# Attention and MoE on one core: work units of 256 queries of two heads, MoE by 256 tokens, routing of two heads packed in 32 rows, and a longer normalisation chain on the Pool queue

## The chip, the core and the metric

The kernel runs on one core of a Trainium2 chip. The core has a matrix engine (TensorE, PE in the profile; its weight loads are listed as PEld), a vector engine (VectorE, DVE), a scalar engine (ScalarE, ACT), a general engine (GpSimd, POOL) and a queue engine (SyncE, SP). Each engine takes its instructions strictly in program order and waits on semaphores of the others, so one waiting instruction holds everything behind it on its engine. SP and POOL also issue DMA transfers. The metric is the device time of one execution in microseconds; of several runs the median is given.

## What is computed

Four batches of eight heads, 768 positions, head size 64. Every query and key is assigned to the nearest of 16 centroids of its head; a query sees only the keys of its own cluster. The result goes through one feed-forward block (512 to 2048 to 512, SiLU) over 3072 tokens.

```python
q_assign = np.argmax(np.einsum('bhsd,hcd->bhsc', q_n, c_n), axis=-1)
k_assign = np.argmax(np.einsum('bhsd,hcd->bhsc', k_n, c_n), axis=-1)
mask = q_assign[:, :, :, None] == k_assign[:, :, None, :]
scores = scale * np.matmul(q, k.transpose(0, 1, 3, 2))
scores = np.where(mask, scores, -1000000000.0)
attn = np.exp(scores - np.max(scores, axis=-1, keepdims=True))
attn = attn / (np.sum(attn, axis=-1, keepdims=True) + 1e-09)
x = np.matmul(attn, v).transpose(0, 2, 1, 3).reshape(B * S, H * D)
h = x @ w_in
g = h * (1.0 / (1.0 + np.exp(-h)))
out = g @ w_out
```

## The kernel before

**Pairs.** Work is cut into 16 pairs: pair p holds two neighbouring heads of one batch, four pairs to a batch. For each pair q and k are loaded (`load_qk`, tiles nat0 and nat1, SP queue), split on DVE into two fp16 halves (`split`, tile hl, lines 109 and 110), and turned by a transposing DMA on the SP queue (`turn`, tile abt, line 115), so that positions lie along the free axis and 128 rows (64 high, 64 low) on the partitions.

**Routing.** `logits` (line 127) multiplies with the normalised centroids, 16 small matmuls a pair, whose results lie in PSUM tiles psL in four strips of 32 partitions (head, q or k), of which 16 rows are used. DVE turns them (`route_a`, lines 136 and 137, tile lt), takes the maximum and the one-hot comparison and turns that back (`route_b`, lines 143 to 149), and writes the scaled one-hot rows into partitions 64 to 80 of abt, over the low half (`route_c`, line 156, four DVE operations a pair). A matmul over 80 rows then gives score plus a large bonus where the clusters agree.

**Attention in slots.** The program is written out in slots. In slot s, `qk` makes the scores of one 128-key block of one head against all 768 queries (lines 167 and 168, PSUM tile st, two buffers) and ACT takes the exponential into P (line 170). Six slots later `pv` multiplies P with the values (line 184); the value tile holds 64 columns of ones beside the values, so the sum of the exponentials z comes out in rows of its own. Half of the 768 queries at a time is accumulated in the one PSUM buffer pv and copied by ACT to osb (line 190). 192 slots make up the attention.

**The z chain.** The sums must divide the result: `z_out` spreads one row of osb over 128 partitions (DMA, tile zt), `z_recip` takes the reciprocal on DVE (line 202) and writes it to DRAM (tile rzd), `z_bcast` reads it back to 64 partitions per head (line 210, tile rzb), and `z_mul` multiplies on DVE into xt (line 216). All DMAs of the chain go on the SP queue, the same as all loads, the transposing DMAs and the stores of the output.

**MoE.** When the four pairs of a batch are done, its 768 tokens are two chunks of 384. `unit_a` (line 230, PSUM tile ph; tanh on ACT, line 234; product on DVE, line 235, tile gt) and `unit_b` (line 244, PSUM tile po; scaling on DVE, line 247, tile ot; store) are put into the slots of the next batch's attention, between `qk` and `pv` and behind `pv`. The last batch's MoE stands behind the attention by itself. psL, ph and po share three PSUM buffers.

The order on every engine is the order in which this Python code emits instructions; `events` puts the routing, loads and z chain of each pair at fixed slots.

## Time and profile before

| | |
|---|---|
| three timings | 468.02, 468.89, 471.84 us, median 468.89 us |
| profiled execution | 473.52 us, of which 471.7 us from first to last instruction |
| PE busy | 358.7 us, 76% |
| ACT busy | 259.5 us, 55% |
| DVE busy | 240.3 us, 51% |
| mean granted clock of TensorE | 0.904 |
| largest shares of the chain that ended last | PE 38%, DMA 23% (rzb 16%), DVE 20%, the SP queue 10% |

A row of instructions reads: line, engine, operation, output<-input, count, busy time, mean of one in ns, idle time of the engine ahead of it and what ended that. A row of stages gives, from A to B, the length, then busy us and instruction counts of PE, PEld, DVE, ACT and POOL, the granted clock (1.00 is full speed), the busy share of the DMA engines and GB/s. In a row of the time line the first number is the start, the second the duration. Matmuls overlap in time, so what a stream of them costs is read from the distance of their starts, not from their durations.

### The profile page before, as it was taken

The numbers are of one execution on the slowest core, as the hardware profiler recorded it, in microseconds if no ns is written. First come the engines' busy times: TensorE is split into PE (matmuls) and PEld (weight loads), VectorE is DVE, ScalarE is ACT, GpSimd is POOL, SyncE is SP. The second block draws the span as 40 slices with busy tenths as digits, with TensorE's granted clock in tenths as the row PEclk, the third lists the DMA queues.
The fourth block names the chain that finished last, engine by engine and source line by source line (L and its number), as shares of the span: only waits on it lengthen the run. The fifth ranks groups of instructions, "written<-read, shape, count | busy, mean of one in ns | idle before, by whom it ended". The sixth has DMA issues, their size and how long they took to land.

```text
span 471.7 us, 5345 instructions
## 1 busy us (share of the span) xinstructions
PE 358.7 (76%) x1922; PEld 179.2 (38%) x1922; DVE 240.3 (51%) x432; ACT 259.5 (55%) x387; POOL 23.6 (5%) x52
## 2 busy tenths in 40 slices
PE   0666474745598795959799596949959899979996
PEld 0122231322254352524354252524425455535552
DVE  7735143618284555645376465636159544536451
ACT  2273563927287373926478382835548688506340
POOL 2123000000000000000000000000000000000000
PEclk9997977979699798979979897998989999988999
DMA  6989956282608063442606154260812310120011
GB/s 176 227 168 218 198 143 143 60 201 35 168 0 200 3 143 105 86 138 56 189 24 155 49 107 139 45 182 24 196 50 42 94 58 23 58 79 24 23 46 67
DMA packets 81067, 48.82 MB, mean 103 GB/s; under 512 B 61072, under 2 KB 75408, under 8 KB 81040
## 3 DMA queue, kind: packets, MB, share of 16 engines
q1 hardware_dynamic: 78352, 44.28, 36.8%
q0 software_dynamic: 2688, 4.19, 5.1%
q8 instruction: 15, 0.25, 0.2%
q14 instruction: 12, 0.10, 0.1%
HBM read 33.59 MB, written 6.39 MB: 85 GB/s over the span
## 4 chain that ended last, share of the span: by engine, by line
PE 38%; DMA 23%; DVE 20%; SPq 10%; ACT 4%; issue 4%; DVEq 0%; ACTq 0%
DMA rzb<-rzd 16%; PE ph L230 13%; PE po L244 12%; PE pv L184 6%; SPq L115 4%; DMA abt<-hl 4%; PE st L167 4%; DVE hl L110 3%; DVE gt L235 3%; DMA zt<-osb 3%; SPq L92 2%; SPq L99 2%; DVE abt L156 2%; PE st L168 2%; DVE hl L109 2%
## 5 line engine op out<-in xcount | busy, mean ns | idle before, releaser
L170 ACT ACTIVATE P<-st,bias_74 128x768 f16<-128x768 f32 x192 | 171.5, 903 | 99.6 <-PE st L168 98.7
L234 ACT ACTIVATE tn<-ph,zbias 128x384 f32<-128x384 f32 x128 | 74.4, 582 | 81.4 <-PE ph L230 80.1
L235 DVE SCALAR_TENSOR_TENSOR gt<-tn,ph 128x384 f16<-128x384 f32 x128 | 69.8, 552 | 75.4 <-ACT tn L234 72.9
L244 PE MATMUL po<-wout_s,gt 128*128 128x512 f16 x384 | 100.4, 393 | 0.0
L230 PEld LDWEIGHTS <-win_s 128*128 128x128 f16 x512 | 52.8, 103 | 90.1 <-issue 59.7
L167 PE MATMUL st<-abt 80*128 80x512 f16 x192 | 80.9, 422 | 1.3 <-ACT P L170 0.5
L230 PE MATMUL ph<-xt_70,win_s 128*128 128x384 f16 x128 | 45.2, 353 | 41.4 <-DVE lt L136 19.5
L168 PE MATMUL st<-abt 80*128 80x256 f16 x192 | 56.4, 294 | 0.0
L127 PE MATMUL psL<-abt,wh 128*32 128x512 f16 (+1 forms) x128 | 21.2, 409 | 45.1 <-DMA abt<-hl 43.6
L244 PEld LDWEIGHTS <-gt 128*128 128x128 f16 x384 | 38.6, 101 | 40.9 <-issue 5.6
L230 PE MATMUL ph<-xt_73,win_s 128*128 128x384 f16 x128 | 45.2, 353 | 6.4 <-DVE xt_73 L216 6.4
L230 PE MATMUL ph<-xt_71,win_s 128*128 128x384 f16 x128 | 45.0, 352 | 0.0
L230 PE MATMUL ph<-xt_72,win_s 128*128 128x384 f16 x128 | 44.9, 350 | 0.0
L190 ACT COPY osb<-pv 128x384 f32<-128x384 f32 x64 | 30.6, 478 | 15.6 <-PE pv L184 15.4
L127 PEld LDWEIGHTS <-wh 128*32 128x32 f16 x128 | 6.2, 105 | 58.8 <-issue 55.4
L167 PEld LDWEIGHTS <-abt 80*128 80x128 f16 x192 | 20.3, 106 | 19.8 <-issue 9.6
L168 PEld LDWEIGHTS <-abt 80*128 80x128 f16 x192 | 20.3, 106 | 17.9 <-issue 9.0
L247 DVE TENSOR_SCALAR ot<-po 128x512 f32<-128x512 f32 x24 | 16.4, 684 | 18.4 <-PE po L244 18.2
L216 DVE TENSOR_TENSOR xt_73<-osb,rzb 64x768 f16<-64x768 f32 x8 | 7.6, 953 | 33.3 <-DMA rzb<-rzd 33.2
L156 DVE TENSOR_SCALAR abt<-oh 16x768 f16<-16x768 f16 x64 | 23.3, 364 | 1.6
L184 PE MATMUL pv<-P,vb_80 128*128 128x384 f16 x72 | 19.7, 359 | 1.6 <-ACT osb L190 1.6
L216 DVE TENSOR_TENSOR xt_72<-osb,rzb 64x768 f16<-64x768 f32 x8 | 7.6, 952 | 24.5 <-DMA rzb<-rzd 24.4
(133 smaller groups left out, 297.0 us busy)
## 6 DMA issues: line engine op xcount, KB each, us to landing
natv<-in_v_dram SPq DMA_DIRECT2D x16, 384.0 KB, 3.9
rzb<-rzd SPq DMA_DIRECT2D x32, 192.0 KB, 5.7
out_dram<-ot SPq DMA_DIRECT2D x24, 256.0 KB, 2.0
win_s<-in_moe_w_in_dram POOLq DMA_DIRECT2D x4, 512.0 KB, 8.6
wout_s<-in_moe_w_out_dram POOLq DMA_DIRECT2D x4, 512.0 KB, 9.1
abt<-hl SPq DMA_TRANSPOSE x32, 3.7
zt<-osb SPq DMA_DIRECT2D x32, 3.0 KB, 2.8
nat_91<-in_q_dram SPq DMA_DIRECT2D x1, 384.0 KB, 2.9
```

Source lines behind the costliest of these rows:

```text
L115: nc.sync.dma_start_transpose(abts[p][:, t], hls[p][:, t].rearrange("p a c d -> p (a c d)"))
L127: nc.tensor.matmul(psL[g : g + 32, 0 : hi - lo], w[:, 2 * r + h], ab[:, h, lo:hi], start=(i == 0), stop=(i == 1),)
L156: nc.vector.tensor_scalar(out=ab[64 : 64 + HC, h, :], in0=ohs[p][g : g + HC, :], scalar1=OHV, scalar2=None, op0=ALU.mult)
L167: nc.tensor.matmul(st[:, 0:512], kt[0:K, ts(j, 128)], qt[0:K, 0:512], start=True, stop=True)
L168: nc.tensor.matmul(st[:, 512:768], kt[0:K, ts(j, 128)], qt[0:K, 512:768], start=True, stop=True)
L170: nc.scalar.activation(out=P, in_=st[:, 0:768], func=AF.Exp, bias=bias32, scale=ESC)
L184: nc.tensor.matmul(po[:, 0:CH], vt[:, j, :], Ps[i, j][:, ts(u, CH)], start=(j == 0), stop=(j == NJ - 1))
L190: nc.scalar.copy(osbs[i][:, ts(u, CH)], po[:, 0:CH])
L230: nc.tensor.matmul(ph[:, 0:CH], win_s[:, r, ts(fb, 128)], xts[r][:, T0 : T0 + CH], start=(r == 0), stop=(r == NR - 1))
L234: nc.scalar.activation(out=tn, in_=ph[:, 0:CH], func=AF.Tanh, bias=zbias, scale=0.5)
L235: nc.vector.scalar_tensor_tensor(out=gts[c][:, fb, :], in0=tn, scalar=1.0, in1=ph[:, 0:CH], op0=ALU.add, op1=ALU.mult)
L244: nc.tensor.matmul(po, gts[c][:, fc, ts(s, 128)], wout_s[:, fc, :], start=(fc == 0), stop=(fc == NFB - 1))
```

## The change

**Units.** One unit is now 256 queries of both heads of a pair: 48 units of three slots, 144 slots. A slot makes two key blocks of two heads against 256 queries: four `qk` matmuls of 256 columns, one exponential over 1024 elements, and two slots later four `pv` matmuls of 256 columns. The copy of the result to osb (512 elements) is on DVE instead of ACT. In batches 1 to 3 the query blocks are the outer loop, so the 256 tokens of a block are complete after four units; batch 0 has an order of its own.

**MoE by 256 tokens.** Twelve chunks of 256 tokens. A `unit_a` covers two blocks of 128 hidden features by 256 tokens (eight matmuls of 256 columns, tanh and product over 512 elements); a `unit_b` is as before, four matmuls of 512 columns. A chunk has eight of each. They are spread over the slots until the next chunk is there; the first is there at slot 36, the last at slot 156.

**Routing.** The two heads' centroids are packed into one strip of 32 columns and accumulated together, so two pairs fill the 128 partitions, and DVE works on two pairs at once over 768 elements instead of 384. Only pairs 0 and 1 are done singly. The scaling by OHV is one DVE operation over the whole tile, and the one-hot rows go into abt by DMAs on the SP queue, four a pair, 64 in all.

**The z chain** runs per unit, 48 times: three DMAs on the POOL queue (144 in place of 80 on SP), the reciprocal three slots behind `z_out`, and `z_mul` nine slots behind it.

Loads and routing are placed earlier (`front`): four pairs of the next batch are made ready during this one, with seven abt buffers for four and six value tiles for three. The weights of the MoE, still on the POOL queue, are issued at slots 8 to 14 and 20 to 26, between the z chain's DMAs.

```diff
-    CH = 384
+    U = 3
+    UQ = S // U
...
-    wh = const.tile([128, H, 32], f16, name="wh")
-    wl = const.tile([128, H, 32], f16, name="wl")
-    NV = 3
...
+    wh = const.tile([128, HB, 2, 32], f16, name="wh")
+    wl = const.tile([128, HB, 2, 32], f16, name="wl")
+    NV = 6
+    vts = [const.tile([128, NJ, 2, 128], f16, name=f"vt{n}") for n in range(NV)]
...
-            abts[p] = mp.tile([128, 2, 2 * NJ, 128], f16, name="abt", bufs=4)
...
+            abts[p] = mp.tile([128, 2, 2 * NJ, 128], f16, name="abt", bufs=7)
...
+            for n, (w, h) in enumerate(((wh, 0), (wh, 1), (wl, 0), (wl, 1))):
+                for a, p in enumerate(pl):
                     for t in range(2):
-                        g = 32 * (2 * h + t)
+                        g = 64 * a + 32 * t
...
-    def route_c(p, h):
-        for t in range(2):
-            g = 32 * (2 * h + t)
-            ab = abts[p][:, t].rearrange("p (h j) c -> p h (j c)", h=2)
-            nc.vector.tensor_scalar(
-                out=ab[64 : 64 + HC, h, :], in0=ohs[p][g : g + HC, :], scalar1=OHV, scalar2=None, op0=ALU.mult
...
+        ohu = mp.tile([128, S], f16, name="ohu", bufs=1)
+        nc.vector.transpose(ohu[0:n], oht[0:n])
         oh = mp.tile([128, S], f16, name="oh", bufs=2)
-        nc.vector.transpose(oh, oht.rearrange("p a c -> p (a c)"))
-        ohs[p] = oh
...
+        nc.vector.tensor_scalar(out=oh[0:n], in0=ohu[0:n], scalar1=OHV, scalar2=None, op0=ALU.mult)
+        ohs[pl[0]] = oh
+
+    def route_c(pl):
+        oh = ohs.pop(pl[0])
+        for a, p in enumerate(pl):
+            for h in range(2):
+                for t in range(2):
+                    g = 64 * a + 32 * t + HC * h
+                    ab = abts[p][:, t].rearrange("p (h j) c -> p h (j c)", h=2)
+                    nc.sync.dma_start(ab[D : D + HC, h, :], oh[g : g + HC, :])
...
-            nc.scalar.copy(osbs[i][:, ts(u, CH)], po[:, 0:CH])
...
-        nc.sync.dma_start(zts[p][:, h, :], osbs[i][row : row + 1, :].rearrange("o (p i) -> o p i", i=NJ))
```

The new functions and the new order of the work:

```python
    def qk(n, s, p, u):
        ab = abts[p].rearrange("p t (h j) c -> p t h (j c)", h=2)
        st = ps.tile([128, 2, 2, UQ], f32, name="st", tag="st", bufs=2)
        for a in range(2):
            for h in range(2):
                nc.tensor.matmul(
                    st[:, a, h, :], ab[0:K, 1, h, ts(2 * s + a, 128)], ab[0:K, 0, h, ts(u, UQ)], start=True, stop=True
                )
        P = mp.tile([128, 2, 2, UQ], f16, name="P", bufs=5)
        nc.scalar.activation(out=P, in_=st, func=AF.Exp, bias=bias32, scale=ESC)
        Ps[n, s] = P
    def pv(n, s, p, u):
        if s == 0:
            pvs[n] = ps.tile([128, 2, UQ], f32, name="pv", tag="pv", bufs=1)
        po = pvs[n]
        P = Ps.pop((n, s))
        for a in range(2):
            for h in range(2):
                nc.tensor.matmul(
                    po[:, h, :], vts[p % NV][:, 2 * s + a, h, :], P[:, a, h, :],
                    start=(s == 0 and a == 0 and h == 0), stop=(s == 2 and a == 1), skip_group_check=True,
                )
        if s == 2:
            osb = mp.tile([128, 2, UQ], f32, name="osb", bufs=6)
            nc.vector.tensor_copy(osb, po)
            osbs[n] = osb
    def z_out(n):
        zt = mp.tile([32, 16], f32, name="zt", bufs=2)
        nc.gpsimd.dma_start(zt, osbs[n][D : D + 1].rearrange("o h x -> o (h x)").rearrange("o (p i) -> o p i", p=32))
        zts[n] = zt
    def z_recip(n):
        rz = mp.tile([32, 16], f32, name="rz", bufs=2)
        nc.vector.reciprocal(rz, zts.pop(n))
        rzd = dr.tile([1, 2 * UQ], f32, name="rzd", bufs=4)
        nc.gpsimd.dma_start(rzd.rearrange("o (p i) -> (o p) i", p=32), rz)
        rzs[n] = rzd
    def z_bcast(n):
        rzb = mp.tile([64, 2, UQ], f32, name="rzb", bufs=2)
        nc.gpsimd.dma_start(rzb.rearrange("p h x -> p (h x)"), rzs.pop(n).to_broadcast([64, 2 * UQ]))
        rzbs[n] = rzb
    def z_mul(n, p, u):
        b, r = divmod(p, HB)
        c = b * U + u
        if c not in xts:
            xts[c] = mp.tile([128, NR, UQ], f16, name="xt", bufs=4)
        osb, rzb = osbs.pop(n), rzbs.pop(n)
        for h in range(2):
            nc.vector.tensor_tensor(
                out=xts[c][D * h : D * h + D, r, :], in0=osb[0:D, h, :], in1=rzb[:, h, :], op=ALU.mult
            )
    def unit_a(c, f):
        if f == 0:
            gts[c] = mp.tile([128, NFB, UQ], f16, name="gt", bufs=2)
        ph = ps.tile([128, 2, UQ], f32, name="ph", tag="moe", bufs=3)
        for e in range(2):
            for r in range(NR):
                nc.tensor.matmul(
                    ph[:, e, :], win_s[:, r, ts(2 * f + e, 128)], xts[c][:, r, :], start=(r == 0), stop=(r == NR - 1)
                )
        tn = mp.tile([128, 2, UQ], f32, name="tn", bufs=3)
        nc.scalar.activation(out=tn, in_=ph, func=AF.Tanh, bias=zbias, scale=0.5)
        nc.vector.scalar_tensor_tensor(
            out=gts[c][:, 2 * f : 2 * f + 2, :], in0=tn, scalar=1.0, in1=ph, op0=ALU.add, op1=ALU.mult
        )
...
    units = []
    for b in range(B):
        if b == 0:
            seq = [(0, 0), (0, 1), (0, 2), (1, 0), (1, 1), (2, 0), (2, 1), (3, 0), (3, 1), (1, 2), (2, 2), (3, 2)]
        else:
            seq = [(r, u) for u in range(U) for r in range(HB)]
        units += [(b * HB + r, u) for r, u in seq]
    LAST = 3 * len(units)
    PVL = 2
...
    def front(pl, R):
        x = R - 26
        for p in pl:
            at(x, lambda p=p: (load(p, 0), load(p, 1)))
            at(x + 3, lambda p=p: load_v(p))
            at(x + 9, lambda p=p: split_turn(p, 0))
            at(x + 11, lambda p=p: split_turn(p, 1))
            at(x + 15, lambda p=p: cast_v(p))
            x += 3
        at(R - 8, lambda: logits(pl))
        at(R - 7, lambda: route_a(pl))
        at(R - 6, lambda: route_b(pl))
        at(R - 5, lambda: route_c(pl))
...
    at(9, lambda: logits([2, 3]))
    at(10, lambda: route_a([2, 3]))
    at(11, lambda: (route_b([2, 3]), route_c([2, 3])))
    for n, fn in enumerate(wl_in):
        at(8 + 2 * n, fn)
    for n, fn in enumerate(wl_out):
        at(20 + 2 * n, fn)
    for b in range(1, B):
        front([b * HB, b * HB + 1], 36 * b - 6)
        front([b * HB + 2, b * HB + 3], 36 * b + 5)
    LAG = 11
    done = {}
    for n, (p, u) in enumerate(units):
        e = 3 * n + 3 + PVL
        at(e, lambda n=n: z_out(n))
        at(e + 3, lambda n=n: z_recip(n))
        at(e + 5, lambda n=n: z_bcast(n))
        at(e + LAG - PVL, lambda n=n, p=p, u=u: z_mul(n, p, u))
        done[p // HB * U + u] = e + LAG - PVL
    avail = {}
    for c in range(NC):
        avail.setdefault(done[c] + 1, []).append(c)
...
    def pop_unit():
        if qa and (not qb or flip[0] % 2 == 0):
            c, f = qa.pop(0)
            unit_a(c, f)
            if f == NFB // 2 - 1:
                qb.extend((c, s, t) for s in range(UQ // 128) for t in range(4))
        elif qb:
            unit_b(*qb.pop(0))
        flip[0] += 1
...
    for s in range(END):
        for fn in events.get(s, ()):
            fn()
        for c in avail.get(s, ()):
            qa.extend((c, f) for f in range(NFB // 2))
        nxt = [x for x in slots if x > s]
        until = (nxt[0] if nxt else END) - s
        acc += left() / (until + 1)
        n = int(acc)
        acc -= n
        if s < LAST:
            m, j = divmod(s, 3)
            qk(m, j, *units[m])
        for _ in range(n - n // 2):
            pop_unit()
        if PVL <= s < LAST + PVL:
            m, j = divmod(s - PVL, 3)
            pv(m, j, *units[m])
        for _ in range(n // 2):
            pop_unit()
    while qa or qb:
        pop_unit()
```

**How instructions move, 1: the queues of the z chain.** On SP before, in the middle of the program (batch 1), the chain's DMAs stand among transposes and loads:

```order
L115 DMA_TRANSPOSE abt<-hl 128x12x128
L204 DMA rzd<-rz 128x2x6
L115 DMA_TRANSPOSE abt<-hl 128x12x128
L99 DMA natv<-in_v_dram 128x2x384
L92 DMA nat_1415<-in_q_dram 128x2x384
L92 DMA nat_1417<-in_k_dram 128x2x384
L210 DMA rzb<-rzd 64x768 x2
L198 DMA zt<-osb 128x1x6
```

On POOL now, about the same place; the numbers are those of the buffers, so that `rzb_1606<-rzd_1535` is seen to wait for the third row:

```order
L185 DMA zt_1459<-osb_1444 32x1x16
L197 DMA rzb_1511<-rzd_1457 64x512
L192 DMA rzd_1535<-rz_1533 32x16
L185 DMA zt_1537<-osb_1528 32x1x16
L197 DMA rzb_1606<-rzd_1535 64x512
```

The chain has left the queue of the loads; on its own queue it takes turns, unit by unit, in the order rzd, zt, rzb.

**2: the start of the POOL queue.** Now, from slot 5 to slot 11 (vt are the value tiles, win_s the first MoE weights):

```order
L185 DMA zt_315<-osb_302 32x1x16
L88 CAST vt2_77<-natv_313 128x6x64 x2
L88 CAST vt3_78<-natv_329 128x6x64 x2
L323 DMA win_s_68<-in_moe_w_in_dram 128x2048
L192 DMA rzd_368<-rz_366 32x16
L185 DMA zt_370<-osb_363 32x1x16
L323 DMA win_s_68<-in_moe_w_in_dram 128x2048
L197 DMA rzb_435<-rzd_368 64x512
L192 DMA rzd_468<-rz_466 32x16
```

Before, POOL held only the value casts and the weights; now the first units' chain stands between them.

**3: DVE in the middle of a batch.** Before, ahead of a routing:

```order
L202 RECIPROCAL rz_1847<-zt_1701 128x12
L109 TENSOR_SCALAR hl_1818<-nat1_1648 128x12x64
L110 SCALAR_TENSOR_TENSOR hl_1818<-nat1_1648,hl_1818 128x12x64
L247 TENSOR_SCALAR ot_1884<-po_1828 128x512
L216 TENSOR_TENSOR xt3_73<-osb_1640,rzb_1890 64x768
L216 TENSOR_TENSOR xt3_73<-osb_1768,rzb_1890 64x768
L136 STREAM_TRANSPOSE lt_1951<-psL_1920 128x512
L137 STREAM_TRANSPOSE lt_1951<-psL_1929 128x256
```

Now, about the same place:

```order
L223 SCALAR_TENSOR_TENSOR gt_1927<-tn_2116,ph_2107 128x512
L179 COPY osb_2141<-pv_2081 128x512
L207 TENSOR_TENSOR xt_1950<-osb_1846,rzb_2023 64x256 x2
L190 RECIPROCAL rz_2145<-zt_2060 32x16
L235 TENSOR_SCALAR ot_2218<-po_2132 128x512
L121 STREAM_TRANSPOSE lt_2225<-psL_2173 128x512
L122 STREAM_TRANSPOSE lt_2225<-psL_2190 128x256
L179 COPY osb_2246<-pv_2162 128x512
L129 TENSOR_REDUCE mx_2248<-lt_2225 128x48
L131 TENSOR_TENSOR oht_2250<-lt_2225,mx_2248 128x768
L136 STREAM_TRANSPOSE ohu_2252<-oht_2250 128x768
L138 TENSOR_SCALAR oh_2254<-ohu_2252 128x768
```

The multiplications of the chain are smaller and stand every third slot, further behind the sums they wait for; the copies osb<-pv, ACT's before, now stand in DVE's row, behind the product gt and between the pieces of the routing.

More of the change, by code (lines that the diff above doesn't have):

```diff
@@ L224, in unit_a @@
-    def unit_a(c, fb):
-        T0 = c * CH
-        if fb == 0:
-            gts[c] = mp.tile([128, NFB, CH], f16, name="gt", bufs=2)
-        ph = ps.tile([128, 512], f32, name="ph", tag="moe", bufs=3)
-        for r in range(NR):
-            nc.tensor.matmul(
-                ph[:, 0:CH], win_s[:, r, ts(fb, 128)], xts[r][:, T0 : T0 + CH], start=(r == 0), stop=(r == NR - 1)
-            )
-        tn = mp.tile([128, CH], f32, name="tn", bufs=3)
-        nc.scalar.activation(out=tn, in_=ph[:, 0:CH], func=AF.Tanh, bias=zbias, scale=0.5)
+        nc.vector.tensor_scalar(out=oh[0:n], in0=ohu[0:n], scalar1=OHV, scalar2=None, op0=ALU.mult)
@@ L371 @@
-    LAST = 12 * NP
-    queue = []
-    NSL = LAST + 14
-    for s in range(NSL):
+    for vt in vts:
+        nc.gpsimd.memset(vt[:, :, :, D:128], 1.0)
+    centroid_math(craw)
+    for p in range(2):
+        for t in range(2):
+            split_turn(p, t)
+        if p == 0:
+            load_v(0)
+            cast_v(0)
+    for t in range(2):
+        load(2, t)
+    logits([0])
+    route_a([0])
+    route_b([0])
+    route_c([0])
+    load_v(1)
+    cast_v(1)
+    wl_in = [lambda r=r: nc.gpsimd.dma_start(win_s[:, r], win_v[:, r]) for r in range(NR)]
```

290 lines of the change are left out of this document (87 added, 203 removed).

## The prediction

> **What bounds the kernel now.** I read the stages first: length, busy us of PE, PEld, DVE, ACT, POOL with instruction counts, granted clock, DMA share, GB/s. The first row lies in the attention of batch 0, the next two are the batches with MoE, routing and loads together, the last is attention with MoE, when nothing is left to load or route.
>
> ```profile
> 20.00:66.00 46.00, 28.66 (x137) 12.51 (x132) 16.29 (x28) 25.70 (x35) 8.25 (x14) 0.85 0.96 204
> ...
> 127.80:233.50 105.70, 86.65 (x477) 43.92 (x477) 57.61 (x102) 64.18 (x96) 3.83 (x8) 0.90 0.41 103
> 233.50:345.40 111.90, 88.94 (x480) 45.00 (x480) 58.31 (x103) 64.33 (x96) 3.85 (x8) 0.89 0.40 100
> ...
> 371.00:407.00 36.00, 34.16 (x197) 18.89 (x196) 17.59 (x32) 29.41 (x45) 0.00 (x0) 1.00 0.14 45
> ```
>
> The reader is to see three things. Until 127.8 us no MoE runs, and neither PE nor ACT is full (28.66 and 25.70 of 46), while DMA is (0.96). In the two middle batches PE is busy 82% and 79%, at a clock of 0.90. Without routing and loads PE is busy 95% at full clock: the engine can do it, the waits keep it from it. The list of waits (who waited for whom, us in total, times, longest) names them:
>
> ```profile
> PE psL L127 <- DMA abt<-hl: 43.6, 19, 6.5
> DVE xt_73 L216 <- DMA rzb<-rzd: 33.2, 4, 10.9
> DVE xt_72 L216 <- DMA rzb<-rzd: 24.4, 4, 10.1
> ```
>
> The time line shows what one wait of DVE does:
>
> ```profile
> 254.30 0.86 SPq L99 DMA_DIRECT2D natv<-in_v_dram  x1
> ...
> 256.30 1.12 SPq L210 DMA_DIRECT2D rzb<-rzd  x2
> 262.37 1.94 DVE L216 TENSOR_TENSOR xt_70<-osb,rzb 64x768 f16<-64x768 f32 x2 [4.47 <-DMA rzb<-rzd]
> 265.11 0.48 PE L230 MATMUL ph<-xt_70,win_s 128*128 128x384 f16 x1 [4.81 <-DVE lt L136]
> 265.39 0.53 PE L230 MATMUL ph<-xt_71,win_s 128*128 128x384 f16 x1
> ...
> 269.59 0.33 PE L230 MATMUL ph<-xt_70,win_s 128*128 128x384 f16 x1
> 269.75 0.32 PE L230 MATMUL ph<-xt_71,win_s 128*128 128x384 f16 x1
> ```
>
> The sums' way back (rzb) is issued behind three loads on SP and lands 6.1 us later. DVE stands, the logits' PSUM buffer isn't emptied, PE stands 4.81 us, and then its matmuls start 0.28 us apart instead of 0.16. So the order of the SP and DVE queues bounds the middle, DMA and SP the start.
>
> **The change, part by part.** The sum has four terms. These rows price them: groups by line (busy us, mean ns of one), then the time line, then the chain that ended last.
>
> ```profile
> L170 ACT ACTIVATE P<-st,bias_74 128x768 f16<-128x768 f32 x192 | 171.5, 903 | 99.6 <-PE st L168 98.7
> ...
> L234 ACT ACTIVATE tn<-ph,zbias 128x384 f32<-128x384 f32 x128 | 74.4, 582 | 81.4 <-PE ph L230 80.1
> L235 DVE SCALAR_TENSOR_TENSOR gt<-tn,ph 128x384 f16<-128x384 f32 x128 | 69.8, 552 | 75.4 <-ACT tn L234 72.9
> L247 DVE TENSOR_SCALAR ot<-po 128x512 f32<-128x512 f32 x24 | 16.4, 684 | 18.4 <-PE po L244 18.2
> L156 DVE TENSOR_SCALAR abt<-oh 16x768 f16<-16x768 f16 x64 | 23.3, 364 | 1.6
> L149 DVE STREAM_TRANSPOSE oh<-oht_86 128x768 f16<-128x768 f16 x8 | 7.8, 978 | 0.3
> L216 DVE TENSOR_TENSOR xt_73<-osb,rzb 64x768 f16<-64x768 f32 x8 | 7.6, 953 | 33.3 <-DMA rzb<-rzd 33.2
> 21.05 6.26 ACT L170 ACTIVATE P<-st,bias_74 128x768 f16<-128x768 f32 x7 [16.43 <-PE st L168]
> 30.83 0.27 PE L168 MATMUL st<-abt 80*128 80x256 f16 x1
> 30.94 0.49 PE L184 MATMUL pv<-P,va_79 128*128 128x384 f16 x2
> ...
> 39.89 1.47 PE psL L127 x12
> ...
> 129.96 1.29 PE ph L230 x4
> ...
> 377.50 0.86 PE po L244 x4
> ```
>
> Scaled by elements, as estimates: DVE has 1.03 ns per element (552 at 384, 684 at 512), so gt and the osb copy of 512 take 0.68 us, an xt of 256 takes 0.42. ACT has 0.84 ns (582 at 384, 903 at 768): an exponential of 1024 takes 1.12 us, a tanh of 512 0.69. Four matmuls of 512 columns take 0.86, so 256 columns cost 0.108 us, and the two rows at 30.8 show one of 256 starting its successor 0.11 us later, with a weight load beside it.
>
> *Term 1, up to slot 36, where MoE begins: 97 us.* The first exponential stood at 21.05. Now a single pair's logits use two strips instead of four (1.47 us cold becomes 2.9), the maximum and comparison grow by 384 elements each (0.8), the scaling shrinks by 1.1, and four DMAs must land (zt below: 2.8): 24.5 us. ACT alone would bring slot 36 at 24.5 + 36 x 1.12 = 65 us. DMA does not:
>
> ```profile
> q1 hardware_dynamic: 78352, 44.28, 36.8%
> q0 software_dynamic: 2688, 4.19, 5.1%
> natv<-in_v_dram SPq DMA_DIRECT2D x16, 384.0 KB, 3.9
> win_s<-in_moe_w_in_dram POOLq DMA_DIRECT2D x4, 512.0 KB, 8.6
> zt<-osb SPq DMA_DIRECT2D x32, 3.0 KB, 2.8
> rzd<-rz SPq DMA_DIRECT2D x16, 6.0 KB, 2.5
> ```
>
> q1 moved 44.28 MB in 36.8% of 471.7 us, 0.255 MB/us. By slot 33 (logits of pairs 6 and 7) eight pairs have been loaded (24 x 0.39 = 9.4 MB) and turned (16 x 0.39 = 6.3 MB): 62 us. The weights took 5.1%, 24 us, and twelve rzb of 131 KB take 6: 92 us at a full share, 95 with three more slots, 97 with gaps. If the second half of the weights (12 us), needed only from slot 38, slips behind, it is 85; the upper end is a rival. Before, the first unit_a stood at 130 (row 129.96).
>
> *Term 2, PE from slot 36 on: 267 us at full clock.* 108 slots x 8 matmuls x 0.108 = 93; 96 unit_a x 8 x 0.108 = 83; 96 unit_b x 0.86 = 83; logits of eight pairs, 16 matmuls each, 1.0 us warm by the half of the row at 39.89 (12 in 1.47, cold): 8. The other two engines have less per batch of 36 slots: PE 74 us; ACT 36 x 1.12 + 24 x 0.69 = 57, against 64.3, since the copies leave it; DVE 58.3 as before + 8.2 for twelve copies + 2.5 for 24 small xt instead of 8 + 2 for reciprocals - 5.8 for line 156 - 4 for two wide routings instead of four - 1 = 60. That the clock is full rests on the row 371 to 407, where no wait is long; at 0.90, as in the middle batches, the term is 296. The row at 265.11 shows what lowers it, a wait of 4.81. The Trainium skill (TensorE: Matmul & The Clock Gate, What's actually happening) puts the limit at about 3.4 us of idleness and the low clock at half; by that rule waits of under 1 us leave the term at 267, and the trace agrees with the half (0.28 against 0.16).
>
> *Term 3, waits in that stretch: 22 us.* The z chain leaves the path: nine slots of 2.07 us are 18.6, and POOL's three issues (0.6 each, row below), 2.8, 0.2, 2.5 and at most 6.1 for rzb make 13.6. What is late next is the copy osb<-pv, for there is one pv buffer. If a unit_a stands just before the closing pv, the slot's exponential, tanh, product and copy end 2.4 us after that unit's last matmul (0.3 + 0.7 + 0.7 + 0.7), while PE has 1.7 us of other work (pv 0.43, qk 0.43, one unit 0.86) before it needs the buffer: a wait of 0.7, in about half of 36 units, 14 us. The routing's second part is one piece of 3.3 us on DVE (maximum and comparison over 768 elements 0.95 each by gt's slope, turn 0.98, scaling 0.4), against three shared PSUM buffers: 1 us each, six times. Late zt: 2. Bounds: 5, if the queues run ahead, and the first rival.
>
> *Term 4, the end: 6 us.* The last chunk's 14 us on PE are in term 2. After the last pv nine slots with one unit in each last 9.6 us, the chain of the last unit by the rows of before's end
>
> ```profile
> 413.11 2.03 DMA zt<-osb
> 415.51 2.37 DMA rzd<-rz
> 417.94 3.11 DMA rzb<-rzd
> ...
> 467.64 0.69 DVE ot L247
> ```
>
> and issues and reciprocal of 2 us takes 9.5: 1 to 2 us late. From the start of ot to the span's end it was 4.1.
>
> POOL's chain has also come behind the value casts, which wait for their loads: from batch 1 on those are issued twelve slots earlier, in slots 6 and 7 one slot, which is among the gaps of term 1. SP loses 80 DMAs of the chain and gets 64 of the one-hot rows; what waits behind those are loads and transposes that are needed at least eight slots later: nothing. More buffers: nothing.
>
> Sum: 97 + 267 + 22 + 6 = 392 us of span. The profiled execution lay 1.8 above its span and the median of the timings 1.0% below that: **390 us**.
>
> **The rivals.** *Waits come back on DVE.* It now holds the copies that release pv, the products that release ph, and the routing in longer pieces, at 60 of 74 us. If PE stays at the 80% of the middle batches, term 2 is 334 and the time 434. For it speaks the single pv buffer; against it that those batches' long waits all begin with rzb. 13%.
>
> *The chain behind the weights.* In slots 8 to 14 and 20 to 26 the three legs of the first units queue behind weights on POOL's one queue, at 8.6 us each: 25.8 against the nine slots' 10.1, so some 16 us late, and 9 more in the second burst: 415. The sum holds the weights' DMA time, not this order. 10%; together with the first rival, 459, 4%.
>
> *Slower: the POOL queue sets the pace.* Per unit it issues rzd, zt, rzb, and the next rzd waits for zt and the reciprocal: 0.6 + 0.6 + landing + 0.2.
>
> ```profile
> 23.83 2.38 POOL L340 DMA_DIRECT2D win_s<-in_moe_w_in_dram  x4
> ```
>
> With zt's 2.8 us this is 4.2, under the 6.2 of three slots. POOL's only transfers in this trace, though, land after 8.6: then 10.0 a unit, 47 x 10.0 + 31 for the first + 27 for the last chunk = 528 of span, 525. It decides from a landing of 4.8 us, and is slower than before from 7.4. I take 2.8, since those transfers carry 512 KB and zt 2 KB: 8%. The Trainium skill (DMA: Bandwidth & Descriptors, SWDGE vs HWDGE vs iDMA) says that POOL's descriptors are written to SBUF and are held up while DVE uses both ports; by that rule an issue could take up to a DVE operation more, and the rows show 0.6 with DVE busy, which leaves the chance as it is.
>
> *Weight loads show.* If each of the 1632 matmuls of 256 columns after slot 36 paid its 0.10 load, 163 us more: 551. The rows at 30.8 speak against it, but never with two in a row: 3%.
>
> **How the numbers follow.** Forecast 62%, own range 363 (term 1 85, term 3 5 to 8) to 404 (12 us more). Then 13, 10, 4, 8 and 3%. The range 364 to 436 holds nearly all of the forecast, the second rival and the first: about 81%. 1% is about what a measurement here can tell. Faster 0.87 (62 + 13 + 10 and half of the 4), same 0.02, slower 0.11.
>
> **What would show it.** Right: unit_a's first matmul near 97 us; no wait of xt on rzb over 2 us after that; PE busy over 90% at a clock above 0.97 from there; PE's waits there mostly at pv on osb, under 1 us each. Wrong: waits of rz on zt or xt on rzb in every unit (POOL's pace), ph waiting for gt at 80% PE (DVE), starts of 256-column matmuls 0.2 us apart (weights), or the first unit_a later than 115 us.

## The result, and the profile after

The changed kernel takes 414.38 us (median of four runs, 413.35 to 424.15) beside 470.37 us for the kernel before on the same chip: a ratio of 0.882, with a 95% interval of 0.875 to 0.889. The forecast was 390 us.

The stages of both kernels, cut at the start of the first `unit_a` (columns: from and to in us, length, busy us and count of PE, PEld, DVE, ACT and POOL, granted clock, DMA share, GB/s). First before:

```profile
20.00:130.00 110.00, 65.81 (x331) 29.92 (x326) 47.32 (x80) 60.68 (x83) 11.13 (x20) 0.84 0.67 150
130.00:471.70 341.70, 288.42 (x1564) 147.77 (x1562) 178.10 (x312) 195.92 (x302) 8.64 (x18) 0.92 0.32 83
```

and then the changed kernel:

```profile
24.00:130.30 106.30, 61.98 (x396) 38.57 (x397) 46.59 (x80) 38.45 (x36) 27.34 (x50) 0.68 0.88 164
130.30:422.40 292.10, 274.67 (x2150) 201.32 (x2147) 182.39 (x337) 177.31 (x205) 67.81 (x132) 0.99 0.36 98
```

The reader is to see that the whole gain lies behind the first `unit_a`. That stretch fell from 341.7 to 292.1 us, with PE busy 94% of it at a clock of 0.99. Of the 49.6 us, 35.9 are PE's idle time (53.3 before, 17.4 now) and 13.7 its busy time. The first `unit_a` itself stands at 130.3 us, where it stood before (130.0), although it should have come at 97. The profiled execution is some 10 us above the median of its runs (that of the rerun below some 6); the variants below have 284 to 290 us behind their first `unit_a` where nothing is changed there, so in a run at the median it would start at about 124 us (an estimate: 414.4 - 1.8 around the span - 289).

What PE waited for behind the first `unit_a` before (130 to 471 us; us in total, times, longest):

```profile
PE ph L230 <- DVE lt L136: 19.5, 5, 5.4
...
PE ph L230 <- DVE gt L235: 12.4, 3, 6.1
PE ph L230 <- DVE ot L247: 9.1, 2, 4.8
```

and what waited for what there in the changed kernel:

```profile
PE pv L173 <- DVE osb L179: 7.5, 10, 1.8
PE ph L218 <- DVE xt L207: 2.6, 1, 2.6
...
DVE xt L207 <- DMA rzb<-rzd: 1.0, 2, 0.8
```

The waits of the products for rzb, up to 10.9 us each before, are gone, and with them PE's long waits for DVE at ph. This is read from the traces: no run took back one part of the change alone, so how much of the 49.6 us is due to the chain's own queue, to its longer distance, to the larger units or to the packed routing is not shown. The time line shows PE there as a gapless stream, four matmuls of 256 columns every 0.44 us, eight in 0.87:

```profile
260.11 0.60 PE L173 MATMUL pv<-P,vt_77 128*128 128x256 f16 x4
260.55 0.60 PE L158 MATMUL st<-abt 80*128 80x256 f16 x4
260.99 1.04 PE L218 MATMUL ph<-xt,win_s 128*128 128x256 f16 x8
```

In the first stage (24 to 130.3 us) the same list reads otherwise:

```profile
ACT P L162 <- PE st L158: 87.0, 19, 20.9
...
PE pv L173 <- DVE osb L179: 31.9, 11, 6.6
...
DVE xt L207 <- DMA rzb<-rzd: 16.9, 4, 7.3
DVE lt L121 <- PE psL L111: 16.3, 3, 6.6
...
PE psL L111 <- DMA abt<-hl: 9.9, 6, 4.6
```

ACT waits for PE, PE for DVE's copy of the sums, DVE for rzb and for logits, the logits for transposes. PE stands 44.3 of the 106.3 us and works the other 61.98 at a clock of 0.68, so at full clock the work would be about 42 us (an estimate: 61.98 x 0.68). That makes the stage 42 us of work, 20 us of low clock and 44 us of waits. What holds it was the question of the experiments.

### The profile page after: what moved, and what is told of

It is laid out like the page before. It is cut to its first block, busy times and chain, and to the rows that moved or that the text cites. A ratio compares the mean times of both kernels' runs of the same rounds, so it can differ in the third digit from the quotient of the medians.

```text
span 422.4 us, 6704 instructions
## 1 busy us (share of the span) xinstructions
PE 340.9 (81%) x2562; PEld 241.7 (57%) x2562; DVE 243.2 (58%) x454; ACT 218.6 (52%) x243; POOL 100.9 (24%) x196
## 4 chain that ended last, share of the span: by engine, by line
PE 50%; DMA 17%; DVE 17%; issue 7%; ACT 3%; SPq 2%; POOL 2%; ACTq 0%; DVEq 0%; POOLq 0%
PE po L232 17%; PE ph L218 12%; PE pv L173 9%; PE st L158 8%; DMA rzd<-rz 7%; DMA abt<-hl 5%; PE psL L111 3%; DVE gt L223 3%; DVE osb L179 3%; DVE hl L93 2%; ACT tn L222 2%; DMA abt<-oh 2%; DVE hl L94 2%; SPq L99 2%; DMA zt<-osb 2%
## 5 line engine op out<-in xcount | busy, mean ns | idle before, releaser
L162 ACT ACTIVATE P<-st,bias_70 128x1024 f16<-128x1024 f32 x144 | 158.6, 1112 | 155.1 <-PE st L158 153.8
L158 PE MATMUL st<-abt 80*128 80x256 f16 x576 | 94.3, 289 | 9.1 <-DMA abt<-oh 8.8
L218 PE MATMUL ph<-xt,win_s 128*128 128x256 f16 x768 | 98.5, 275 | 3.7 <-DVE xt L207 2.6
L223 DVE SCALAR_TENSOR_TENSOR gt<-tn,ph 128x512 f16<-128x512 f32 x96 | 63.7, 670 | 41.1 <-ACT tn L222 40.9
L222 ACT ACTIVATE tn<-ph,zbias 128x512 f32<-128x512 f32 x96 | 65.6, 684 | 36.6 <-PE ph L218 36.6
L192 POOL DMA_DIRECT2D rzd<-rz x48 | 25.5, 531 | 150.1 <-DVE rz L190 149.9
L179 DVE COPY osb<-pv 128x512 f32<-128x512 f32 x48 | 32.9, 685 | 31.8 <-PE pv L173 31.8
L197 POOL DMA_DIRECT2D rzb<-rzd x48 | 25.7, 535 | 104.5 <-DMA rzd<-rz 100.4
L207 DVE TENSOR_TENSOR xt<-osb,rzb 64x256 f16<-64x256 f32 x96 | 39.6, 413 | 18.6 <-DMA rzb<-rzd 17.9
L173 PE MATMUL pv<-P,vt_77 128*128 128x256 f16 x108 | 19.1, 307 | 10.3 <-DVE osb L179 10.3
L173 PE MATMUL pv<-P,vt_75 128*128 128x256 f16 x108 | 18.1, 295 | 9.5 <-DVE osb L179 9.5
L173 PE MATMUL pv<-P,vt_78 128*128 128x256 f16 x108 | 17.5, 288 | 9.9 <-DVE osb L179 9.9
L173 PE MATMUL pv<-P,vt_76 128*128 128x256 f16 x108 | 17.5, 288 | 7.1 <-DVE osb L179 7.1
```

Source lines behind the costliest of these rows:

```text
L158: nc.tensor.matmul(st[:, a, h, :], ab[0:K, 1, h, ts(2 * s + a, 128)], ab[0:K, 0, h, ts(u, UQ)], start=True, stop=True)
L162: nc.scalar.activation(out=P, in_=st, func=AF.Exp, bias=bias32, scale=ESC)
L173: nc.tensor.matmul(po[:, h, :], vts[p % NV][:, 2 * s + a, h, :], P[:, a, h, :], start=(s == 0 and a == 0 and h == 0), stop=(s == 2 and a = ...
L179: nc.vector.tensor_copy(osb, po)
L192: nc.gpsimd.dma_start(rzd.rearrange("o (p i) -> (o p) i", p=32), rz)
L197: nc.gpsimd.dma_start(rzb.rearrange("p h x -> p (h x)"), rzs.pop(n).to_broadcast([64, 2 * UQ]))
```

## The experiments

Each run is compared with the kernel before, on the same chip. The changed kernel, run again without an edit, is the control.

> The changed kernel once more, as the measure for the others of this call. Both theories: 412 to 417 us. The first unit_a stood at 133 us in the profile after, and that execution was 10 us longer than the timed ones; if those 10 us lie in the first stage (up to the first unit_a), it stands near 123 here, if they lie behind it, at 133 again with a stretch of about 279 behind it instead of 289.

It measured 416.41 us, a ratio of 0.883 (0.875 to 0.891), with the first `unit_a` at 130.0 us in its profile and 290.3 us behind it. (The 133 us of this expectation is a misreading; the first `unit_a` of the changed kernel starts at 130.3.)

### Order or volume

Two runs take the chain's legs out from behind the weights, two leave the weights out. First, all eight weight transfers ahead of the z chain:

```diff
-    for n, fn in enumerate(wl_in):
-        at(8 + 2 * n, fn)
-    for n, fn in enumerate(wl_out):
-        at(20 + 2 * n, fn)
+    for fn in wl_in + wl_out:
+        at(0, fn)
```

> All eight weight loads are issued at slot 0, ahead of the first unit's chain; nothing else changes, so the same bytes move. Theory A, order (the small DMAs of the chain stand behind weights in POOL's one queue, 8 to 9 us each time, one unit after the other): the first unit's chain lands late, near 70 us, all later ones in 2 to 3 us a leg; first unit_a at about 105, 395 to 402 us. Theory B, volume (DMA is busy 0.85 of the first stage and any order costs the same): first unit_a where it was, 412 to 418 us.

It measured 418.82 us, 0.890 (0.883 to 0.896), the first `unit_a` at 129.6 us. Between 24 and 60 us of this run (KB each, median us from issue to landing):

```profile
wout_s<-in_moe_w_out_dram POOLq DMA_DIRECT2D x4, 512.0 KB, 19.3
...
abt<-hl SPq DMA_TRANSPOSE x3, 15.2
```

The chain no longer met weights later, but the loads and transposes of pairs 2 and 3 met all of them now. The split of pair 2 waited 21.62 us for its q, the copy osb stood behind it on DVE, and PE waited 20.0 us for that copy. Later, between 60 and 97 us, zt and rzd landed after 4.4 and 3.5 us, against 5.7 and 5.8 in the control and 7.2 and 7.7 in the first profile of the changed kernel. What was won there was lost here.

Second, the three legs of the chain of batch 0's twelve units on the SP queue:

```diff
-        nc.gpsimd.dma_start(zt, ...)
+        (nc.sync if n < 12 else nc.gpsimd).dma_start(zt, ...)
...
```

> The chain's three DMAs go to the SP queue for the 12 units of batch 0, POOL keeps the weights and the later units. Theory A: no leg stands behind a weight any more, but they stand behind SP's loads and its waits; legs of 3 to 5 us instead of 8 to 9, first unit_a at 105 to 115, 392 to 405 us. Theory B: 412 to 418 us. A third outcome, 420 or more, would say that SP's own waits cost as much as the weights.

It measured 421.17 us, 0.892 (0.884 to 0.900), the first `unit_a` at 130.6 us. That is the third outcome that was named ahead. The chain did not land quickly on SP either: between 60 and 97 us zt took 5.0 us and rzd 5.2 (5.7 and 5.8 in the control), though no weight stood ahead of them on that queue. POOL, freed of the chain, then waited for the value loads in its casts. So neither run bears out that the chain standing behind weights on one queue, the prediction's second rival, costs the 33 us.

Third, no weight transfers at all. A first version had POOL fill the weight tiles in their place:

```diff
+    nc.gpsimd.memset(win_s, 0.01)
+    nc.gpsimd.memset(wout_s, 0.01)
     centroid_math(craw)
...
```

> The weights of the MoE are not loaded; POOL fills both tiles with a constant at the start, so the output is not the reference's. Takes away both the order and the 24 us of DMA time. Theory A: legs of 2 to 3 us, first unit_a at 95 to 103, 380 to 388 us, not much under e1 and e2. Theory B: the same, but then e1 and e2 stay at 412 to 418.

It measured 417.59 us, 0.887 (0.882 to 0.892), but says little: the fill, 13.9 us on POOL, held back the start, the first exponential came about 13 us later (38.8 us), and the first `unit_a` at 128.2 us. From the first exponential to the first `unit_a` it was thus 89.4 us, against 104.8 in the changed kernel. The next version lets ACT fill the tiles while it has nothing to do:

```diff
+    for c in range(NR):
+        nc.scalar.activation(out=win_s[:, c], in_=bias32.to_broadcast([128, DF]), func=AF.Copy, scale=-0.0005)
+        nc.scalar.activation(out=wout_s[:, 4 * c : 4 * c + 4].rearrange("p c d -> p (c d)"), ...)
...
```

> The weights are not loaded, and this time ACT, which is idle until 25 us, fills the tiles with a constant, so that the start isn't delayed as by POOL's fill (there the first exponential stood at 39 instead of 25 us). The output is not the reference's. Theory C, preparation (the first stage is a serial row of load, split, transpose, logits and routing per pair, which PE's queue waits for in order, at the low clock): what was left of the stage without weights, 90 us for 36 slots, stays; first unit_a at 115, 400 to 404 us. Theory A or B (weights, by order or volume): first unit_a at 95 to 103, 380 to 390 us.

It measured 402.95 us, 0.852 (0.848 to 0.856), the first `unit_a` at 115.9 us, as theory C had it. Its first stage:

```profile
24.00:115.90 91.90, 57.69 (x396) 36.92 (x397) 46.73 (x80) 38.01 (x36) 21.28 (x42) 0.72 0.64 144
```

Against 414.4 and 416.4 us the weights cost 11 to 13 us (some 14 by the ratios to the kernel before). Without them small transfers land in about half the time or less. In the changed kernel, between 60 and 97 us:

```profile
abt<-oh SPq DMA_DIRECT2D x8, 24.0 KB, 5.8
rzd<-rz POOLq DMA_DIRECT2D x4, 2.0 KB, 7.7
zt<-osb POOLq DMA_DIRECT2D x4, 2.0 KB, 7.2
abt<-hl SPq DMA_TRANSPOSE x4, 8.8
```

and in the kernel without weights in the same window:

```profile
abt<-oh SPq DMA_DIRECT2D x14, 24.0 KB, 2.2
rzd<-rz POOLq DMA_DIRECT2D x6, 2.0 KB, 2.8
zt<-osb POOLq DMA_DIRECT2D x6, 2.0 KB, 2.6
abt<-hl SPq DMA_TRANSPOSE x5, 5.1
```

In the control's profile the same four rows are 6.8, 5.8, 5.7 and 6.8 us, so the first set is at the upper end of what this kernel shows. Yet the stage is only some 14 us shorter in the profile, and DMA is now idle a third of it (0.64). The weights explain under half of the 33 us; the rest is waits that are there without them too (PE stands 91.90 - 57.69 = 34.2 us).

### Moving one step of the preparation

If the row is load, split, transpose, logits, routing of one pair after another, an earlier load should help. Pair 3's q and k are issued right behind the first routing instead of in slot 4:

```diff
     route_c([0])
+    load(3, 0)
+    load(3, 1)
     load_v(1)
...
-    at(4, lambda: (load(3, 0), load(3, 1)))
```

> q and k of pair 3 are loaded right behind the first pair's one-hot rows instead of in slot 4, where on SP they stand behind the second pair's one-hot rows and two transposes; nothing else changes. Theory C: DVE waited 7.3 us for this load and PE 12.4 us in all at the logits of pairs 2 and 3; 5 to 8 us less, 407 to 411 us. Theory A or B: the chain's legs behind the weights take it up again, 412 to 418 us.

It measured 413.1 us, 0.875 (0.870 to 0.879), which its interval does not quite separate from the control; the first `unit_a` stood at 125.1 us. The other way, batch 1's logits and routing, which stand in this stage too, five and three slots later:

```diff
...
-        at(R - 8, lambda: logits(pl))
-        at(R - 7, lambda: route_a(pl))
...
+        at(R - 8 + d, lambda: logits(pl))
+        at(R - 7 + d, lambda: route_a(pl))
...
-        front([b * HB, b * HB + 1], 36 * b - 6)
-        front([b * HB + 2, b * HB + 3], 36 * b + 5)
+        front([b * HB, b * HB + 1], 36 * b - 6, 5 if b == 1 else 0)
+        front([b * HB + 2, b * HB + 3], 36 * b + 5, 3 if b == 1 else 0)
```

> Logits and routing of batch 1's pairs, 14 and 9 slots ahead of their first use, stand 5 and 3 slots later, so that PE's queue does not wait for their transposes in the middle of batch 0. Theory C: the waits of 9 and 14 us in front of them shrink by about the slots that now stand ahead, 5 to 8 us each; 402 to 410 us. Theory A or B: the waits move to the z chain, 412 to 418 us.

It measured 420.18 us, 0.888 (0.883 to 0.893): no gain. PE's waits for transposes fell to 1.9 us (24 to 130 us), and its waits for osb rose to 38.8. Both edits together:

> Both of the two edits. Theory C: their gains add, 396 to 404 us. Theory A or B: 410 to 418 us.

416.54 us, 0.881 (0.877 to 0.884), the first `unit_a` at 118.8 us. The earlier start of MoE was not kept: the stretch behind it took 296.7 us, and the postponed logits and routing had still to be done there. An early first `unit_a` therefore counts only together with the time of the run. Theory C had forecast 407 to 411, 402 to 410 and 396 to 404 us for these three runs and missed each time; that the row of preparation sets the stage is therefore not shown by moving its steps.

### PE's longest wait: the copy osb

One of PE's longest waits for osb in the first stage is this piece of the changed kernel's time line:

```profile
97.23 0.60 PE L158 MATMUL st<-abt 80*128 80x256 f16 x4
98.22 0.24 DVE L190 RECIPROCAL rz<-zt 32x16 f32<-32x16 f32 x1 [1.65 <-DMA zt<-osb]
98.39 0.88 DVE L129 TENSOR_REDUCE mx<-lt 128x48 f32<-128x768 f32 x1
...
102.17 0.96 DVE L94 SCALAR_TENSOR_TENSOR hl<-nat_542,hl 128x768 f16<-128x768 f32 x1
103.05 0.68 DVE L179 COPY osb<-pv 128x512 f32<-128x512 f32 x1
103.79 1.01 PE L173 MATMUL pv<-P,vt_78 128*128 128x256 f16 x4 [5.96 <-DVE osb L179]
```

The copy that frees the one pv buffer stands on DVE behind a reciprocal that waits for zt, a routing and a split, and PE stands 5.96 us. Two edits take the copy off DVE, for batch 0's twelve units or for all 48:

```diff
-            nc.vector.tensor_copy(osb, po)
+            if n < 12:
+                nc.scalar.copy(osb, po)
+            else:
+                nc.vector.tensor_copy(osb, po)
```

```diff
-            nc.vector.tensor_copy(osb, po)
+            nc.scalar.copy(osb, po)
```

> For the first twelve units (batch 0) the copy of the sums out of PSUM (osb) is made by ACT, which is idle most of that stage, and no longer by DVE; everything else stays. In the profile of the changed kernel PE waits 31.9 us in 11 for osb between 24 and 133.4 us, because the copy stands on DVE behind splits, routing and products that themselves wait for loads, reciprocals and broadcasts, and there is one pv buffer. Theory D (that single buffer, drained on DVE's queue, is what stretches the first stage): these waits fall below 8 us, the first unit_a comes at 105 to 113 us, and the time is 388 to 400 us. Theory C (the row of preparing pairs sets the stage, whatever order the copy has): PE then waits for the transposes and the routing strips in place of osb, the first unit_a stays behind 122 us, and the time is 406 us or more. If ACT is disturbed by the copies, the exponentials would show it by new waits of PE for P.

> The copy osb is on ACT for all 36 units, the same in the first stage as with the first twelve. Behind the first unit_a this puts 24 x 0.69 = 16 us more on ACT, which has 219 us of work in 422, and takes it from DVE; the waits for osb there were 7.5 us in 10. Theory D: 385 to 398 us, at or up to 7 us below the kernel with ACT in the first twelve alone. If Term 3 was right in that DVE's bursts cost PE something in the later stage, this run is a few us faster than that one; if ACT's tanh and exponentials are in the way, as slow or slower. Theory C: 403 us or more.

(The second text counts 36 units; the program has 48, so behind the first twelve 36 copies move and not 24.) The first measured 411.44 us, 0.874 (0.867 to 0.881), the second 407.72 us, 0.864 (0.855 to 0.873). For the first stage theory D falls, and theory C's forecasts came true. With the copy on ACT in the first twelve units (24 to 123.2 us):

```profile
PE psL L111 <- DMA abt<-hl: 29.1, 10, 7.7
...
PE pv L173 <- ACT osb L180: 8.4, 10, 0.9
...
PE st L158 <- DMA abt<-oh: 6.8, 2, 5.9
...
24.00:123.20 99.20, 54.86 (x395) 35.38 (x396) 43.39 (x74) 43.22 (x47) 27.48 (x50) 0.79 0.85 176
```

The waits for osb fell from 31.9 to 8.4 us as meant, and PE stands 99.20 - 54.86 = 44.3 us, no less than before the edit (44.3, and 42.7 in the control): what it no longer waits at pv it waits at the logits, for transposes, and at the strips. Only the clock is better (0.79), and with it PE's busy time.

The second run says more of the stretch behind. Both programs have the same order up to the first `unit_a`, at 123.2 and 128.2 us (so 5 us is what this place varies by), and behind it:

```profile
123.20:408.10 284.90, 271.27 (x2150) 200.06 (x2148) 178.50 (x330) 177.71 (x206) 67.84 (x132) 1.00 0.37 100
```

with the copies of the other units on DVE, and with all on ACT:

```profile
128.20:405.20 277.00, 270.23 (x2150) 200.53 (x2147) 158.67 (x294) 193.75 (x242) 69.72 (x132) 1.00 0.38 103
```

7.9 us less, with PE idle 6.8 us instead of 13.6. In the changed kernel the waits for osb there add up to 7.5 us. ACT's busy time rose by 16.0 us (193.75 - 177.71), the figure forecast, but by luck: 36 copies at 0.45 and not 24 at 0.69. The medians of the two runs differ by 3.7 us with overlapping intervals, so the size is not settled by them. Against the control (0.883) the kernel with all copies on ACT is faster, with intervals that do not touch, and it is the best complete kernel of these runs: 407.72 us.

The early load added to the first of the two edits:

> The copy by ACT for the first twelve units, and q and k of pair 3 loaded right behind the first routing, as in the run that came to 413.1 us. Theory D: with the osb waits gone, the loads and transposes of pairs 2 and 3 are the next in line, so the early load is worth its 3 us or more again: 383 to 396 us, first unit_a at 100 to 110 us. Theory C: 403 us or more, with the early load the only gain.

410.09 us, 0.873 (0.867 to 0.878), the first `unit_a` at 121.2 us: nothing that can be told from 0.874.

### Everything at once

Since no single move took much from the sum of the waits, the last run made all of them:

```diff
+            nc.scalar.copy(osb, po)
...
+    load(3, 0)
+    load(3, 1)
...
+            at(x + 9 + d, lambda p=p: split_turn(p, 0))
+            at(x + 11 + d, lambda p=p: split_turn(p, 1))
...
+    at(12, lambda: cast_v(2))
+    at(13, lambda: cast_v(3))
...
+        d = 4 if n < 7 else 0
+        at(e + 3 + d // 2, lambda n=n: z_recip(n))
+        at(e + 5 + d // 2, lambda n=n: z_bcast(n))
+        at(e + LAG - PVL + d, lambda n=n, p=p, u=u: z_mul(n, p, u))
...
```

> Everything that was found waiting in the first stage is moved at once: osb copied by ACT for all units, q and k of pair 3 loaded early, logits and routing of batch 1 five and three slots later and its splits with them, the v casts of pairs 2 and 3 on the Pool queue six slots later (they held the z chain's issues for up to 17.9 us), and for the first seven units two slots more before the reciprocal and the broadcast and four before the products. Theory E (several causes in series, each hidden behind the next, so that moving one alone is worth little): the first unit_a comes at 100 to 112 us instead of 128.2 with the ACT copy alone, PE's waits there for transposes, strips and sums together fall from about 50 us to below 30, and the time is 385 to 398 us. Theory F (the latency from one load to the strips, and PE at its low clock, hold the stage, and no order of these steps helps): first unit_a behind 120 us and 402 to 412 us, as with the ACT copy alone.

It measured 432.38 us, 0.923 (0.912 to 0.935): longer than any other run of these, outside both forecasts. Theory E is refuted, and theory F's 402 to 412 us was missed as well. The first `unit_a` came at 140.8 us. Transfers between 60 and 97 us and PE's main waits up to 140.8 us of this run:

```profile
wout_s<-in_moe_w_out_dram POOLq DMA_DIRECT2D x3, 512.0 KB, 15.0
...
abt<-hl SPq DMA_TRANSPOSE x3, 12.8
PE psL L111 <- DMA abt<-hl: 40.1, 9, 11.1
...
PE st L158 <- DMA abt<-oh: 12.8, 2, 11.9
```

With the casts no longer in the way, POOL issued the first two weight transfers at 34.6 and 38.3 us (53.5 and 55.1 with the ACT copy alone), beside the loads and transposes of pairs 2 and 3. Between 60 and 97 us a transpose then took 12.8 us to land, instead of 7.9 with the ACT copy alone. That the one comes from the other is argued; which of the five moves did it was not separated.

What the runs leave open: what the first stage's shortest time is. None brought its `unit_a` below 115.9 us. That PE's low clock lengthens the row is argued from the rows (a slot costs PE 1.7 us there, four matmuls in 0.85 twice, against 0.87 at full clock) but no run raised the clock alone. Routing strips written by an engine instead of a DMA, as before the change, were not tried.

## Why the prediction was right in direction and wrong in its first term

**The step that failed is term 1: "92 us at a full share, 95 with three more slots, 97 with gaps".** The first `unit_a` came 33 us later than that in the profile (some 27 in a run at the median), past the 115 us named as the mark of a wrong forecast. The bytes were right: the parts of the term make 21.5 MB (9.4 + 6.3 + 4.2 + 1.6), and the changed kernel moved 21.9 by then (185 and 164 GB/s before and after 24 us). Two parts were too small. One is the time for these bytes: the changed kernel's share of 0.88 makes 106.3 x 0.88 = 93.5 us of full-share time from 24 us on, and 24 x 0.74 = 17.8 lie ahead, together 111 and not 92. The same sum for the control, whose stage is as long at a share of 0.80, gives 106.0 x 0.80 + 24 x 0.75 = 103. Term 1 took 0.255 MB/us from the whole program, but the row of before at 20 to 66 us that the prediction shows has 204 GB/s at a share of 0.96, which is 0.21 and would have made about 101 us of the same bytes. Without the weights the sum is 91.9 x 0.64 + 24 x 0.72 = 76, so the weights took 27 to 35 us, not 24. (The share is a rough measure: between 60 and 97 us of the changed kernel it reads 1.09.) The other part is the gaps: 19 to 27 us, not 2, and in the kernel without weights 116 - 76 = 40. The view that misled was the row of before at 20 to 66 us with DMA at 0.96 and PE and ACT at some 60%. It was read as a full resource that bounds the stage by its volume. The experiment without weights shows that volume alone does not: with a third of the DMA time free the run became only 11 to 13 us shorter. What is left are waits along load, split, transpose, logits, strips and chain, which follow each other on in-order queues; that this row sets the stage is argued from the lists of waits, and the runs that moved its steps did not bear it out one by one. The forecast summed DMA by volume and ACT by work, and never the row. A sign of it stood in the prediction's own list of waits: of the 43.6 us that PE waited for transposes before, only 2.5 lie behind 130 us, so nearly all of them belong to the first stage and not to the middle of the program, for which the list was read:

```profile
PE psL L127 <- DMA abt<-hl: 2.5, 5, 0.7
```

The first exponential, 24.5 us by the forecast, came at 25.44; the terms given for it add up to 25.0.

**Terms 2 to 4 held.** 267 + 22 + 6 = 295 us were forecast from slot 36 on; the row 130.30:422.40 has 292.1, with PE busy 274.67, and the variants that leave this stretch alone have 284 to 290. The estimates by elements came out in the groups of the page of the changed kernel (busy us, mean ns of one):

```profile
L162 ACT ACTIVATE P<-st,bias_70 128x1024 f16<-128x1024 f32 x144 | 158.6, 1112 | 155.1 <-PE st L158 153.8
...
L223 DVE SCALAR_TENSOR_TENSOR gt<-tn,ph 128x512 f16<-128x512 f32 x96 | 63.7, 670 | 41.1 <-ACT tn L222 40.9
L222 ACT ACTIVATE tn<-ph,zbias 128x512 f32<-128x512 f32 x96 | 65.6, 684 | 36.6 <-PE ph L218 36.6
...
L179 DVE COPY osb<-pv 128x512 f32<-128x512 f32 x48 | 32.9, 685 | 31.8 <-PE pv L173 31.8
...
L207 DVE TENSOR_TENSOR xt<-osb,rzb 64x256 f16<-64x256 f32 x96 | 39.6, 413 | 18.6 <-DMA rzb<-rzd 17.9
```

1.12, 0.68, 0.69, 0.68 and 0.42 us were forecast. In term 3 the wait of pv for osb was the right one and its size right (0.75 us each against 0.7), but it stood in 10 units and not in half of 36: 7.5 us of the 14 (18 x 0.7 is 12.6, so 14 was a little high to begin with). The clock there is 0.99. Two other sums are off by little: the legs of the chain make 13.4 us and not 13.6, and in term 4 a chain of 9.5 us beside nine slots of 9.6 would not be late. The Trainium skill (TensorE: Matmul & The Clock Gate, What's actually happening), with its gate of about 3.4 us of idleness, was used for the statement that waits under 1 us leave the clock alone; the trace agrees behind the first `unit_a`, with 0.99. It was not applied to the first stage, where PE waited 3 to 7 us at a time and the clock was 0.68.

**The rivals.** DVE taking the place of rzb (434 us) did not come where it was placed: PE is busy 94% there. It came in the first stage, as 31.9 us of waits for osb, and there it was only one link of the row. The chain behind the weights (415 us) hit the time and not the cause: its legs do land late (7.7 and 7.2 us), but moving them or the weights gained nothing, so that the time agrees is luck. POOL's pace is refuted by the median landings over the whole run, all under the 4.8 us from which it would decide, with issues of 0.51 to 0.54 us each; only in the first stage were they longer (zt 7.2 us between 60 and 97 us):

```profile
rzb<-rzd POOLq DMA_DIRECT2D x48, 128.0 KB, 2.9
...
zt<-osb POOLq DMA_DIRECT2D x48, 2.0 KB, 1.8
rzd<-rz POOLq DMA_DIRECT2D x48, 2.0 KB, 2.1
```

Weight loads do not show: the gapless stream at 260 us has a matmul of 256 columns every 0.11 us, each with its load.

The range held the time because the second rival's 415 us and the first's 434 us were in it; the likeliest case's own range, which ended at 404, did not. That the measured time is inside is therefore partly luck.

## What to carry to other kernels

A stage with a nearly full DMA and half-busy engines is not thereby bound by volume: take a large transfer out in thought and ask what is late next, and add up the latencies of the row that prepares the first pieces beside the volume. Where several in-order queues feed each other, moving one wait can leave their sum as it was (42.7 and 44.3 us of idle PE with the osb waits, 41.0 to 49.8 in the three runs with the copy on ACT and little else moved), and moving all of them cost more than it gained (432.38 us). In the full pipeline the opposite held: there the terms by counts and durations, 295 us, came within 3 us of the first profile and within 11 of the others.

## What the runs showed of the hardware that was not expected

The clock of TensorE was also seen to fall after waits of under 3 us, and after PE was at work again. The changed kernel, run again, shows it:

```profile
35.47 0.60 PE L173 MATMUL pv<-P,vt 128*128 128x256 f16 x4 [2.67 <-DVE osb L179]
35.91 1.01 PE L158 MATMUL st<-abt 80*128 80x256 f16 x4
36.71 1.06 PE L173 MATMUL pv<-P,vt 128*128 128x256 f16 x4
37.56 1.06 PE L158 MATMUL st<-abt 80*128 80x256 f16 x4
```

The first four matmuls behind the 2.67 us took 0.44 us, the next ones 0.80 and 0.85, though PE had no further wait. In the first profile of the changed kernel a wait of 2.88 us at the same place was followed by a granted clock of 0.50 (35.5 to 38.0 us), where it had been 1.00 (29.0 to 32.4 us). The Trainium skill (TensorE: Matmul & The Clock Gate, What's actually happening) describes a window of 3413 ns that runs freely; a window that ends while PE has just resumed would look like this, but these rows do not show where windows lie.

Landings grew with what was queued beside them. A transposing DMA's median landing was 5.0 to 5.1 us without weights (60 to 134 us), 6.8 and 8.8 in the two profiles of the changed kernel (60 to 97 us), 12.8 in the run with all moves (60 to 97 us), and 15.2 with all weights ahead (24 to 60 us). The 2 KB transfers of the chain grew by a larger factor: zt from 2.6 us without weights to 5.7 and 7.2 with them.
